# Reciprocal rows spread by transfers, and a rounded query copied by a transfer

## The chip, the cores and the metric

The kernel runs on one core of a Trainium2 chip. The metric is the device time of one execution in microseconds (us), lower is better; the median of several runs is given, and one further execution is profiled.

## The reference, cut to what matters

Three blocks follow each other: decayed causal attention, a mixing block with a two-dimensional Fourier transform and a feed-forward layer, and a second mixing block. The change touches the attention alone, where each row is divided by the sum of its exponentials:

```python
B, H, S, D = 4, 8, 576, 64
scores = scale * np.matmul(q, k.transpose(0, 1, 3, 2))
decay = cum[:, :, :, None] - cum[:, :, None, :]
scores = np.where(causal, -1000000000.0, scores + decay)
scores = scores - np.max(scores, axis=-1, keepdims=True)
attn = np.exp(scores)
attn = attn / (np.sum(attn, axis=-1, keepdims=True) + 1e-09)
out = np.matmul(attn, v)
```

All of it is in 32-bit floats. The 32 pairs of batch and head are the "heads" below; two neighbours make a "pair" (16 pairs).

## The kernel before

**Stages.** `phase1` does the attention and the Fourier transforms of the four batches, `phase2` the feed-forward layer in groups of weights, `phase3` the last block. Where accuracy needs it, a value is split into a rounded high part and a low rest, and the products of the parts are added up in PSUM.

**One head of phase 1.** `load_head` brings raw (128 x 2 x 576: key and query, each twice, on partitions 0 to 63 and 64 to 127) by SP. `prep_units` makes what the score product needs: ACT casts raw into hi; ACT casts the query half of raw into q2 (L251; the tile is called q in the rows), 64 x 576; POOL subtracts twice, for the low part of the query (into hi, L253) and of the key (into kl, L255). Partitions 64 and 65 of q2 and kl carry the decay. `score_units` then does, for each of five blocks of query rows, two matmuls into a bank of PSUM (hi with hi, then q2 with kl), a masked minimum on DVE and an exponential on ACT, which also gives the row sums zs. `turn_units` transposes the exponentials on PE (P to PT), and `av_units` multiplies them by v for both heads of a pair, into one PSUM tile T (pt in the rows) whose partitions 0 to 63 belong to the first head and 64 to 127 to the second; rows of T are features, columns are the 576 queries.

**The division.** With the last block of a pair's second head, ACT adds 1e-9 to the sums, DVE takes the reciprocal rz (128 x 2 x 5), and POOL spreads it to a tile wide, 128 x 5 x 128 (each value 64 times). After the product with v, `spread` turns wide by five transposes on PE, into two banks of PSUM, and ACT copies these in two pieces (448 and 128 columns) to R, 128 x 576, of which there is one buffer. `evac_pair` multiplies T by R on DVE, into X for an even pair and Y for an odd one. After an odd pair one-row transfers (x<-Y, Y<-Y, Y<-x) put the middle features in place; sums and differences of X and Y go to `fft_units` after every fourth pair.

**Order.** `phase1` records the calls up to the turn of the last head and then issues them in an order written out as a string (`ORDERS`), which pins the order of the instructions on each engine, transfers among them. All recorded instructions show as L71 in the trace. What follows is ordered by the framework: the turn of the last head, the spreads of the last two pairs (L326, L327), the last Fourier transform and the first weight loads of phase 2 (L587). Every engine works its own queue in order. SP gives out nearly all transfers of this stage, and a transfer that waits for its input holds those behind it.

Of the kernel before, what the change touches and what calls it, by code (L numbers as in the profile page):

```python
# [8 lines left out]
F32 = mybir.dt.float32  # L9
# [4 lines left out]
ALU = mybir.AluOpType  # L14
# [3 lines left out]
B, H, S, D = 4, 8, 576, 64  # L18
# [4 lines left out]
HT = S // 2 + 1  # L23
# [3 lines left out]
TOP = (0, 66, 192, 320, 448)  # L27
END = (66, 192, 320, 448, 576)
# [25 lines left out]
G = 4  # L54


def f(ap):
    return ap.bitcast(F32)
# [29 lines left out]
class Net:  # L88
# [150 lines left out]
    def prep_units(self, n, pair, raw, hd):  # L239
        nc = self.nc  # L240
        g = n % 2
        kl, q2 = pair["kl"], self.q2[g]
        hi = self.w2.tile([128, 2, S], F32R, tag="hi", name="hi")
        hd["hi"] = hi
        if n == 0:
            nc.scalar.copy(hi[:, 1], raw[:, 1])
            nc.scalar.copy(hi[:, 0], raw[:, 0])
        else:
            nc.scalar.copy(hi, raw)
        yield  # L250
        nc.scalar.copy(q2[0:64], raw[0:64, 1])  # L251
        lows = nc.vector if n == 0 else nc.gpsimd
        lows.tensor_tensor(hi[64:128, 1], raw[64:128, 1], f(hi[64:128, 1]), ALU.subtract)  # L253
        yield
        lows.tensor_tensor(kl[0:64, g], raw[0:64, 0], f(hi[0:64, 0]), ALU.subtract)  # L255
        yield

    def score_units(self, hd, g):
        nc = self.nc
        hi, kl, q2 = hd["hi"], hd["pair"]["kl"], self.q2[g]  # L260
        P = self.P[hd["g"] % 2]
        mn = self.w3.tile([128, 8], F32, tag="mn", name="mn", bufs=2)
        pr = hd["g"] // 2
        zs, rz = self.zs[pr % 2], self.rz[pr % 2]
        hd["P"] = P
        for i in (4, 3, 2, 1, 0):
            end, m0 = END[i], 448 - TOP[i]
            q = slice(TOP[i], TOP[i] + 128)
            ps = self.bank_a()
            pd = self.bank_a() if i == 4 else None  # L270
            parts = [(ps, 0, 448), (pd, 448, end)] if i == 4 else [(ps, 0, end)]
            with self.tc.high_priority(20):
                for t, a, b in parts:
                    nc.tensor.matmul(t[:, 0 : b - a], hi[:, 1, q], hi[:, 0, a:b], start=True, stop=False)
                    nc.tensor.matmul(t[:, 0 : b - a], q2[:, q], kl[:, g, a:b], start=False, stop=True)
                p = P[:, POFF[i] : POFF[i] + end]
                lowest, least = mn[:, i : i + 1], 3.0e38
                for t, a, b in parts:
                    if b < end:
                        to = mn[:, 5:6]  # L280
                    else:
                        to = lowest
                    nc.vector.tensor_tensor_reduce(  # L283
                        out=p[:, a:b], in0=t[:, 0 : b - a], in1=self.mask[:, m0 + a : m0 + b],
                        scale=-0.125, scalar=least, op0=ALU.add, op1=ALU.min, accum_out=to,
                    )
                    least = to
                nc.scalar.activation(p, p, AF.Exp, bias=lowest, scale=-1.0, accum_out=zs[:, g, i : i + 1])
            if i == 0 and g:
                nc.scalar.activation(rz, zs, AF.Copy, bias=1e-9)  # L290
                nc.vector.reciprocal(rz, rz)
                wide = self.w3.tile([128, 5, 128], F32, tag="wide", name="wide", bufs=1)
                each = rz.rearrange("p g i -> p i g").unsqueeze(3).to_broadcast([128, 5, 2, 64])
                nc.gpsimd.tensor_scalar(
                    wide.rearrange("p i (g c) -> p i g c", g=2), each, 1.0, 1.0, ALU.mult, ALU.mult
                )
                hd["pair"]["rz"] = wide
            yield

    def turn_units(self, hd):  # L300
# [18 lines left out]
    def spread(self, p, T, wide):  # L319
        nc = self.nc  # L320
        R = self.c1.tile([128, S], F32, tag="R", name="R", bufs=1)
        for ps, some in ((self.bank_b(), range(4)), (self.bank_a(), (4,))):
            c0 = TOP[some[0]]
            for i in some:
                n = END[i] - TOP[i]
                nc.tensor.transpose(ps[:, TOP[i] - c0 : END[i] - c0], wide[0:n, i], self.ident[0:n, 0:n])  # L326
            nc.scalar.copy(R[:, c0 : END[some[-1]]], ps[:, 0 : END[some[-1]] - c0])  # L327
        return R

    def av_units(self, m, hds, T, wide, done):  # L330
# [733 lines left out]
    def phase3(self):  # L1064
# [58 lines left out]
DIGITS = "#$%&()*+,-./0123456789:;<=>?@ABCDEFGHIJKLMNOPQRSTUVWXYZ[]^_`abcdefghijklmnopqrstuvwxyz|"  # L1123
ORDERS = (
    (
        "&~$6~+X~,e~,e~,e~,e#*35=2)297*+1%)~$$).&|+%/.#$+##///#)-%+(*#)#**#$3<-=[#-811$.T5%;0..252~*p~*p.3361"
        "5#;;4#;*:8,#1>6#*&w;w*()P&***&&l+00G#&.,d+..//,AE=#CJJ?$-@-;-C$,,,,4,,,,,,$+J0##%#$00#%%@2>i#i#%f0%9"
        "#$77:0]/&4//::2/$.?68=#CC/;00-@@>+-0<0./3?#?W,#(,#tu*&&**o.33()H4h#./13#.I&?GN$M@A0C00$F////7//://$."
        "..M#%#$&#G%2$1#%%5%>2=#A&&&9$81(6%00>B#=2//B:A#G,F?/-/=C+@A#,,-FG111)1++#>8#&;&*,,,*+#1+4516#$JCC/4A"
        "4%3@3333%22226222X#)9)$33++O71$5%66&()))6#A6$?D)#((%3(33&(1533$:>:20@$7>-DD./;0,:@@3=..D<D.$//X$)#-5"  # L1130
        "#9(&7)+++)I50#024#$&II$BC,0=$////>/8/<//$.....P$#$##$$$=0#/11%A%%#2D&<<$%%2&#11&F0422=$<1#,A9@-F9E@/"
        "=+.B,A?--G>#F,11]#;@+#&A=--//&.(M+,N&#2:::(18888%>#66H%55555+@5#b))77^,$7#**2*827%)7#6))%=)$G*&:)C,)"
        "F)&8>#=)<77C&B9$55H>+FMM46D26+II$F4::D$7.1),/41,5-4>D?4`BB43@$???$*=-$;pp,oo:n#.l3)620G1e*2.2/1$^)G&"
        "*EX,S((9P+9++#&)#(((&&.&%%%/%%%d#%8%%_%66$5(##%HT,Y0,,22O]$+$$$##+++#*,,$+P#*1**())#5&4#?%2(((<M()%("
        "((C&B&)))&(/-~(Y.^&-GG-&,,FF+-&,,,//*.#-%*++#N*&))C&B)(((&.^*--$,%%**S&)3)00t%(.*R**(lB%&*?(EE&***$S"
        ")8DD99$88(:6>>997@(Q((3(($&&0&&/-&&&&(&7#6FE66?6>%,,3,-?%7=*>%*-**7+++)*A)@BBU)*#)K)))(**P**H())#(#&"
        "%,%&+&&:(9*8**&)#(%$%%J%$$G%x*%%$>s&=&$((9((LHH$MM6NN66&P55b55$>K444@66?6864JJ4IZZI5444Q5PD;;4:9?499"
        "Q9EK4:I8N7M8NN877C7$<J;;C;;J6I;HH;:::GAwwA~%5<?3$~%1>$$~%.0$$9$2$O$$M$$$$+$u#B$(@)F*E>+$D***(9c98AAG"
        "G)77:K_::~$RJ8))$(83((((00((/1W-(((((=)#;&:#9D9FC%..6..%.;.E.%?/>-,CCEE/;,...2<0#=0A-@@D@/$.6111.N%M"
        "74%3.56,52QUCTDc#b/Q1L$__0u+Z%>&)<)D*B)))5)=&((((G%&&&&&&&k:%$0%%%%%%()//#$&&+&$%(#+H+$**D*%)$(($)Z)"  # L1140
        ")$#&7$7%%*$))$(F)(G(&**@$%%*&))%((I%&&3&@%?(((<(@%?-&#X+***DD$)~(8)0+3+++$++(*I+H($FF&&&&E&.&?&&&&;~"
        "$(&(*$T)z%(P((&&&&.&(((&M&?)>E&D****9EE$O999)8;7$>>997@(Q((3((((1$&&/-&&&&(&7#6E66?B6>%,,3,-?%7=*%*-"
        "**78<<+)**))BBK6++)**#)=BGB(A***,,(++)*##(%+&1&&,%+K,*I&#*$%F(($&&A%%$s$$$9%nAA%$$$4>MM4NN6$5eP55886"
        "7773H645444:K_K;4II554V64PPD4:9488>9948DJ:LI8N7M8NN777C7=<<D<3;EJ6I;HH;:::GAA<?3$``~$^>$$0$$38$$O$N$"
        "$$$,$$y#B$(@)*++K<+$*CCi(==8HHLL);;A~$+OcAA~$&N<)~$#)$(73((((/55((6/X(((((A(#?N?#>G>F*%33:3+3E>1C+D5"
        "1110CC110090II22;2#X11/222_W0VVV*RR<$]Q]$l.k-NX|hz~$1-~$0t#JvT#p~$5HR~$3o5G`++#h)C99dIVIIn%xHHHH#GGG"
        "GUGGG/$$-~$W$$$$$$---$,#+N+$###&#/~$8P&%%%#$$~$0$&G#~$C%%%C%+%#$$&&#%#$$$#q%~$.#$$%%#########~$)&&#%"
        "%%$$$$$))$((($&&&&$(I((I(((DD(($A&+++=++++++C&6AH&GM$L**$1))&)))&()&&&&&&,---#,/&.*66-#$$*(+&&#4%3+/"
        "/&%#--+E(+C)/*..E)D),HH;-#,,+++&*2***4**7***7/#5))%((-/)#(($%#$#%%%%##"
    ),  # L1150
)

# [118 lines left out]
```

## Time and profile before

| what | us |
|---|---|
| median of 3 runs | 929.73 |
| lowest and highest | 927.27 to 930.9 |
| the profiled execution's own time | 927.5 |
| its span in the trace | 925.7 |
| attention stage in the written order (L71), ends at about | 231 |
| last Fourier transform, until about | 274 |

The rows below come from the profiled execution. PE is TensorE's matmuls, PEld its weight loads, DVE VectorE, ACT ScalarE, POOL GpSimd, SP SyncE; SPq is the queue from which SP gives out transfers. A row of instructions reads: line, engine, operation, tile written <- tiles read, sizes. Times in brackets are idle time of the engine just before, with what ended it.

### The profile page before, as it was taken

The numbers are of one execution on the slowest core, as the hardware profiler recorded it, in microseconds if no ns is written. First come the engines' busy times: TensorE is split into PE (matmuls) and PEld (weight loads), VectorE is DVE, ScalarE is ACT, GpSimd is POOL, SyncE is SP. The second block draws the span as 40 slices with busy tenths as digits, with TensorE's granted clock in tenths as the row PEclk, the third lists the DMA queues.
The fourth block names the chain that finished last, engine by engine and source line by source line (L and its number), as shares of the span: only waits on it lengthen the run. The fifth ranks groups of instructions, "written<-read, shape, count | busy, mean of one in ns | idle before, by whom it ended". The sixth has DMA issues, their size and how long they took to land.

```text
span 925.7 us, 15855 instructions
## 1 busy us (share of the span) xinstructions
PE 888.4 (96%) x5960; PEld 839.1 (91%) x5960; DVE 604.6 (65%) x1495; ACT 417.7 (45%) x1014; POOL 329.5 (36%) x369
## 2 busy tenths in 40 slices
PE   4999999999698999999999999999999999999998
PEld 3777888878597999999999999999999999999998
DVE  9776787857989635456653665446787747657563
ACT  6898897885535223223221322223335435334331
POOL 6677887987203443000000000000036526435330
PEclk9999999999799999999999999999999999999999
DMA  5743333330323100022232222313300010010001
GB/s 168 217 140 108 121 129 107 110 104 15 110 84 113 47 1 1 4 79 66 80 109 74 91 91 90 142 62 132 100 27 2 1 39 14 14 40 1 26 28 52
DMA packets 23725, 68.04 MB, mean 74 GB/s; under 512 B 2906, under 2 KB 6362, under 8 KB 23648
## 3 DMA queue, kind: packets, MB, share of 16 engines
q1 hardware_dynamic: 20608, 62.88, 20.7%
q0 software_dynamic: 2320, 2.97, 1.2%
q10 hardware_dynamic: 720, 1.18, 0.4%
q8 instruction: 47, 0.77, 0.3%
q14 instruction: 30, 0.25, 0.1%
HBM read 57.91 MB, written 9.07 MB: 72 GB/s over the span
## 4 chain that ended last, share of the span: by engine, by line
PE 58%; DVE 9%; ACT 2%; issue 1%; DMA 0%; POOL 0%; ACTq 0%; DVEq 0%; SPq 0%
PE pa L788 19%; PE pb L802 11%; PE po L802 8%; PE pa L1020 5%; PE pb L1009 5%; PE pa L973 4%; PE po L1009 3%; DVE kra L980 1%; DVE kra L983 1%; DVE kra L982 1%; DVE kra L981 1%; DVE kra L997 1%; DVE kra L979 1%; DVE u L810 1%; PE pa L969 1%
## 5 line engine op out<-in xcount | busy, mean ns | idle before, releaser
L788 PE MATMUL pa<-un,wf 128*128 128x384 f32 x1152 | 220.3, 340 | 7.3 <-ACT un L776 4.4
L788 PEld LDWEIGHTS pa<-un,wf 128*128 128x128 f32 x1152 | 203.7, 191 | 10.4 <-ACT un L776 5.3
L794 DVE SCALAR_TENSOR_TENSOR h<-pa,h 128x384 fp32r<-128x384 f32 x96 | 52.3, 555 | 140.4 <-ACT h L793 140.4
L802 PE MATMUL pb<-h,wf 128*128 128x384 f32 x660 | 133.8, 336 | 0.3 <-DVE u L810 0.3
L802 PEld LDWEIGHTS pb<-h,wf 128*128 128x128 f32 x660 | 116.1, 188 | 1.2 <-DVE u L810 1.0
L793 ACT ACTIVATE h<-pa 128x384 fp32r<-128x384 f32 x96 | 45.7, 489 | 134.2 <-PE pa L788 131.4
L802 PE MATMUL po<-h,wf 128*128 128x384 f32 x492 | 105.4, 339 | 0.4
L965 POOL COPY xd<-u 128x64 f32<-128x64 f32 x32 | 7.3, 266 | 263.7 <-DVE u L810 253.7
L1009 PE MATMUL pb<-wtk,z 128*128 128x288 f32 x513 | 98.3, 295 | 1.6 <-ACT z L998 1.6
L71 ACT ACTIVATE P<-P,mn 128x576 f32<-128x576 f32 (+4 forms) x155 | 86.4, 559 | 16.3 <-DVE mn L71 16.2
L802 PEld LDWEIGHTS po<-h,wf 128*128 128x128 f32 x492 | 86.2, 188 | 3.6 <-ACT h L793 1.5
L999 POOL TENSOR_TENSOR z<-kra,z 128x256 fp32r<-128x256 f32 x72 | 53.2, 753 | 93.8 <-ACT z L998 93.7
L71 PE MATMUL pb<-ident,P 128*128 128x128 f32 (+2 forms) x465 | 81.8, 285 | 4.5 <-DVE PT L71 2.3
L1009 PEld LDWEIGHTS pb<-wtk,z 128*128 128x128 f32 x513 | 79.3, 188 | 2.3 <-ACT z L998 2.3
L71 DVE CUSTOM_DVE_ANT_0 P<-pa,mask 128x448 f32<-128x448 f32 (+3 forms) x155 | 66.3, 454 | 20.3 <-PE pa L71 17.1
L1009 PE MATMUL po<-wtk,z 128*128 128x288 f32 x351 | 75.1, 295 | 0.8 <-ACT z L998 0.8
L71 PE MATMUL pa<-hi 128*128 128x448 f32 (+1 forms) x186 | 65.4, 367 | 1.0 <-DVE mn L283 0.5
L71 PEld LDWEIGHTS pb<-ident,P 128*128 128x128 f32 (+2 forms) x465 | 56.0, 145 | 11.1 <-DVE PT L71 3.9
L973 PE MATMUL pa<-wf,xs 128*128 128x256 f32 x456 | 64.1, 289 | 0.0
L71 DVE COPY PT<-pb 128x448 f32<-128x448 f32 (+1 forms) x93 | 52.9, 594 | 11.7 <-PE pb L71 10.5
L1009 PEld LDWEIGHTS po<-wtk,z 128*128 128x128 f32 x351 | 57.3, 188 | 1.2 <-ACT z L998 1.2
L973 PEld LDWEIGHTS pa<-wf,xs 128*128 128x128 f32 x456 | 57.1, 190 | 0.0
(281 smaller groups left out, 1667.1 us busy)
## 6 DMA issues: line engine op xcount, KB each, us to landing
raw<-in_qk SPq DMA_DIRECT2D x31, 576.0 KB
raw<-in_wf SPq DMA_DIRECT2D x32, 512.0 KB
raw<-in_wtk SPq DMA_DIRECT2D x18, 288.0 KB
v<-in_vp SPq DMA_DIRECT2D x16, 320.0 KB
out<-ob SPq DMA_DIRECT2D x12, 288.0 KB
dft<-in_dft POOLq DMA_DIRECT2D x8, 346.0 KB, 4.8
raw<-in_wth SPq DMA_DIRECT2D x4, 512.0 KB
st_wth<-raw SPq DMA_DIRECT2D x4, 512.0 KB
```

The source lines that it names most:

```text
L71: getattr(getattr(self.nc, engine), name)(*a, **kw)
L788: nc.tensor.matmul(ps[:, 0:CH], t[:, l, 128 * d : 128 * d + 128], un[r][:, d], start=n == 0, stop=n == 11)
L793: nc.scalar.activation(h[:, 0], ps[:, 0:CH], AF.Relu)
L794: nc.vector.scalar_tensor_tensor(h[:, 1], ps[:, 0:CH], 0.0, f(h[:, 0]), ALU.max, ALU.subtract)
L802: nc.tensor.matmul(outs[d], t[:, l, 128 * d : 128 * d + 128], h[:, r], start=k % G == 0 and n == 0, stop=k % G == G - 1 and n == 2,)
L810: nc.vector.tensor_tensor(u[:, d], outs[d], u[:, d], ALU.add)
L969: nc.tensor.transpose(xt[:, 128 * k : 128 * k + 128], src, self.ident)
L973: nc.tensor.matmul(th, xs[:, l, d], self.wth[d][:, r, 256 * hf : 256 * hf + 256], start=n == 0, stop=n == 11)
L979: nc.vector.tensor_scalar(kk, th, INV2PI, MAGIC, ALU.mult, ALU.add)
L999: nc.gpsimd.tensor_tensor(z[:, 1], t, f(z[:, 0]), ALU.subtract)
L1009: nc.tensor.matmul(acc[k][th], z[:, l, 128 * k : 128 * k + 128], self.wtk[kt][:, r, 288 * th : 288 * th + 288], start=first and i == 0 and ...
L1020: self.nc.tensor.matmul(ps[:, 0:288], self.wch[d][:, l, 128 * eo : 128 * eo + 128], us[d][:, r, sl], start=d == 0 and n == 0, stop=d == 3 ...
```

## The change

For every head from the third on, the query half of q2 is no longer cast by ACT but copied by a transfer from hi, on SP. The reciprocals of a pair are transposed once on PE (128 x 10 to 10 x 128), copied by ACT out of PSUM and stored to DRAM by SP as two rows of 640, one per head; POOL's tile wide goes. `spread` is then six transfers on SP from DRAM to R: for each of the two heads, three ranges of columns (66, 126 and 384), each row sent to 64 partitions. The written order is a new string; it covers the new calls.

```diff
-        nc.scalar.copy(q2[0:64], raw[0:64, 1])
+        if n < 2:
+            nc.scalar.copy(q2[0:64], raw[0:64, 1])
+        else:
+            nc.sync.dma_start(f(q2[0:64]), f(hi[0:64, 1]))
...
                 nc.vector.reciprocal(rz, rz)
-                wide = self.w3.tile([128, 5, 128], F32, tag="wide", name="wide", bufs=1)
-                each = rz.rearrange("p g i -> p i g").unsqueeze(3).to_broadcast([128, 5, 2, 64])
-                nc.gpsimd.tensor_scalar(
-                    wide.rearrange("p i (g c) -> p i g c", g=2), each, 1.0, 1.0, ALU.mult, ALU.mult
-                )
-                hd["pair"]["rz"] = wide
+                ps = self.bank_a()
+                nc.tensor.transpose(ps[0:10, 0:128], rz.rearrange("p g i -> p (g i)"), self.ident)
+                turned = self.w3.tile([10, 128], F32, tag="wide", name="rt", bufs=2)
+                nc.scalar.copy(turned, ps[0:10, 0:128])
+                rows = self.fdram.tile([2, 640], F32, tag="rows", name="rows", bufs=2)
+                nc.sync.dma_start(rows.rearrange("g (i q) -> (g i) q", i=5), turned)
+                hd["pair"]["rz"] = rows
...
     def spread(self, p, T, wide):
         nc = self.nc
         R = self.c1.tile([128, S], F32, tag="R", name="R", bufs=1)
-        for ps, some in ((self.bank_b(), range(4)), (self.bank_a(), (4,))):
-            c0 = TOP[some[0]]
-            for i in some:
-                n = END[i] - TOP[i]
-                nc.tensor.transpose(ps[:, TOP[i] - c0 : END[i] - c0], wide[0:n, i], self.ident[0:n, 0:n])
-            nc.scalar.copy(R[:, c0 : END[some[-1]]], ps[:, 0 : END[some[-1]] - c0])
+        for i, n in ((0, 66), (1, 126), (2, 384)):
+            for g in range(2):
+                each = wide[g : g + 1, 128 * i : 128 * i + n].to_broadcast([64, n])
+                nc.sync.dma_start(R[64 * g : 64 * g + 64, TOP[i] : TOP[i] + n], each)
         return R
...
 ORDERS = (
     (
-        "&~$6~+X~,e~,e~,e~,e#*35=2)297*+1%)~$$).&|+%/.#$+##///#)-%+(*#)#**#$3<-=[#-811$.T5%;0..252~*p~*p.3361"
...
+        "&~$8~+_~,l~,l~,l~,l#*35=2)29*+14*%).&+%z/z.#%+#$*&)$//()//%,<-#;E%1#$0:[55#<##U..8.#1611#30-15#40,*#"
...
     ),
 )
```

## Rows read from the trace of the kernel before

**Rows 1.** Busy time, share and instructions of each engine, from the page.

```profile
PE 888.4 (96%) x5960; PEld 839.1 (91%) x5960; DVE 604.6 (65%) x1495; ACT 417.7 (45%) x1014; POOL 329.5 (36%) x369
```

**Rows 2.** Busy time by stretch: span, each engine's busy us (count), clock, DMA.

```profile
31.10:66.30 35.20, 34.29 (x268) 26.71 (x266) 25.05 (x96) 31.69 (x90) 25.43 (x22) 1.00 0.61 183
...
25.00:225.00 200.00, 194.29 (x1521) 162.16 (x1520) 143.68 (x518) 163.32 (x466) 159.90 (x146) 1.00 0.37 118
...
225.00:250.00 25.00, 17.40 (x119) 12.68 (x117) 22.23 (x49) 15.06 (x36) 9.63 (x12) 0.79 0.25 85
...
300.00:925.70 625.70, 619.22 (x4028) 613.23 (x4026) 370.24 (x791) 201.76 (x442) 137.86 (x171) 1.00 0.16 52
```

**Rows 3.** Instruction groups, 25 to 225 us: busy us, mean ns, idle before.

```profile
L71 ACT CAST q<-raw 64x576 fp32r<-64x576 f32 x29 | 19.2, 663 | 0.0
...
L71 ACT COPY R<-pb 128x448 f32<-128x448 f32 x14 | 7.3, 520 | 3.7 <-PE pb L71 3.7
...
L71 ACT COPY R<-pa 128x128 f32<-128x128 f32 x14 | 3.8, 268 | 7.6 <-PE pa L71 5.7 <-DVE Y L71 1.9
...
L71 POOL TENSOR_SCALAR wide<-rz 128x640 f32<-128x640 f32 x15 | 10.9, 726 | 9.4 <-DVE rz L71 6.8 <-DVE mn L71 1.9 <-ACT P L71 0.7
...
L71 PE MATMUL pb<-ident,wide 128*128 128x128 f32 (+2 forms) x56 | 10.0, 266 | 0.2
...
L71 PE MATMUL pa<-ident,wide 128*128 128x128 f32 x14 | 4.2, 303 | 0.0
```

**Rows 4.** Timeline of PE: start, us, instructions merged.

```profile
219.92 1.26 PE L71 MATMUL pb<-ident,P 128*128 128x128 f32 x10 [0.20 <-DVE u L71]
```

**Rows 5.** Waits of PE and of its weight loads, 25 to 225 us: us, times, longest.

```profile
PE pb L71 <- ACT PT L71: 1.3, 2, 0.7
...
PE pb L71 <- ACT P L71: 1.2, 3, 0.8
...
PEld pb L71 <- ACT P L71: 2.1, 4, 1.0
...
PEld pb L71 <- ACT PT L71: 1.1, 2, 0.9
```

**Rows 6.** Timeline of ACT and POOL around one head's cast.

```profile
123.64 1.15 ACT L71 CAST hi<-raw 128x1152 fp32r<-128x1152 f32 x1
...
124.91 1.43 POOL L71 TENSOR_TENSOR hi<-raw,hi 64x576 fp32r<-64x576 f32 x1 [0.21 <-POOL u L71]
...
126.42 1.42 POOL L71 TENSOR_TENSOR kl<-raw,hi 64x576 fp32r<-64x576 f32 x1
```

**Rows 7.** Timeline of SP, which gives out transfers, 123 to 140 us.

```profile
123.87 4.32 SPq L71 DMA_DIRECT2D raw<-in_qk  x2
...
134.06 0.51 SPq L71 DMA_DIRECT2D x<-Y  x1
...
135.75 0.33 SPq L71 DMA_DIRECT2D raw<-in_qk  x1
...
136.24 0.51 SPq L71 DMA_DIRECT2D Y<-Y  x1
...
139.69 0.25 SPq L71 DMA_DIRECT2D Y<-x  x1
```

**Rows 8.** Timeline of the hand-over: SP, DVE and ACT, 228 to 241 us.

```profile
228.99 8.18 SPq L587 DMA_DIRECT2D raw<-in_wf  x3
...
230.49 0.22 DVE L71 RECIPROCAL rz<-rz 128x10 f32<-128x10 f32 x1 [0.24 <-ACT rz L71]
...
232.59 0.67 ACT L601 ACTIVATE a<-raw 128x512 f32<-128x512 f32 x1 [0.99 <-DMA raw<-in_wf]
...
237.29 0.75 DVE L364 TENSOR_TENSOR Y<-pt,R 128x576 f32<-128x576 f32 x1
...
238.07 0.50 SPq L378 DMA_DIRECT2D x<-Y  x1
...
240.48 0.50 SPq L379 DMA_DIRECT2D Y<-Y  x1
```

More of the change, by code (lines that the diff above doesn't have):

```diff
@@ L1125 @@
     (
-        "&~$6~+X~,e~,e~,e~,e#*35=2)297*+1%)~$$).&|+%/.#$+##///#)-%+(*#)#**#$3<-=[#-811$.T5%;0..252~*p~*p.3361"
[L1127 to L1149, printed above, removed]
+        "&~$8~+_~,l~,l~,l~,l#*35=2)29*+14*%).&+%z/z.#%+#$*&)$//()//%,<-#;E%1#$0:[55#<##U..8.#1611#30-15#40,*#"
@@ new lines @@
+        "7,6/,,55#2),91(#7#(%#%%%H4$(~*L~*L--C-))),$+)=*<$)8>>_E$D8(Y$%BBU5575%P6%28L%8$$H0$:$$,0$6$5.$3-$1$="
+        "+$$$,##;#..#--99(,N(N2~$;~$<2+((#.)(22(&2&&44#&&+&#00%%,(&5+&$3*%)H4/$.D(-))j)$++>)*<$)?8>]E$D$X<7%6"
+        "AAR?66&$M63%%I8$$<0$$$,0$66$.$-2>$,$$$$##;#..#>>--(,(2((2)1#&(&446&,&&+#**,*#+(--$..71((()/*.$.&%,,/"
+        "*+AjA.h+---<Db%C=I<H%+::&(DTD8:8)O>)M5)<6&@(3(((/(2(81$&&.?&-&$%%#$$//$.<.)-)4#3+((807)#((3((+66#%(("
+        "(#22&&.()-))$8&0%0G++$*00$/B/$@)-%($8^$%88Y88>%U==85:P7%99L%5%I%14%$$=/$$,$+$*$$$$$$$#28=2+11,,,#+4,"
@@ new lines @@
+        "..#2552+#+6)5))::#-+,,,00//-+#(,--&#4(#3)%*Y,%--0**+A$@-*,,<,$B;;@J$I*9`%&7F[F:77=V=?=6(Q7<(%M&43&I1"
+        "&?&&.&<.$%,%+%%)%%=6&##333.2..9);8/-$#.3,::--+,/0#:-9.#088--03C002*#78+X+2Y2)A+AA/+>$P~$?P==#~$;<<~$"
+        "9);~$7;%:#9~$29~$1999$888&#,,,%+++++#006*55/444*5344#8,#00#&#1111#00&$)%#&&)$33**(%//#<C&%B,:~).??#+"
+        "-<--+,,7,#++*..#-,8)7+#+++++(@@#2.17(#-4--52-CC&0#**#)??<.)<-*++****))0,$++(E(=7=(;;~$&,)+(|*6*S*(P."
+        ".)0-$(+l,(()@g@Ke-(,,a,B)AGG:;;;;>N<)<9;>><+C**7*$)643((((/(.(-(=,((((1#00>0=+/+66.++:39,&++#4**-%@("
@@ new lines @@
+        "*>*%#((;;9M)%))))33)&(#+F++&&&<++&*&)T%(&%%%$))))$$&Bu//C%%$$n<$**j;;$g::%EcE$FJ6I]7==7?<76CCA:6G&5$"
+        "7JDI4HH:6645%E5%@$$$=$/$-$F,$+C$4*$$$$$)#(0((>11(#,55#%,%#$$44;y.)w~%7)(22~%3(/(~%0*6.)$~%+333$&b4%%"
+        "FFt/++q+//,%-k-?<C%<AHH%;+_:&H(GY9:8)$(7;Q(3=%E&&1&&.&22=&0&$%.%%%%*>#$($33#22-1-#,<,7),5$*-*:#9+/++"
+        "0#/-.0.#1+33)44//,/504.+#2370(H5555SS~$765+%3B3#~$/2)1~$,11~$*%0$~$&//~$$////($#000%//4///177/$/###&"
+        "*55#4BB4AA#&?&$%#..($&&,,#)%0<0)$.?$?//-.$-#,,+M1+-/~(n0#/F*,#0,//#.--+,,,#(5,#++)*&/=/#;%AA%#KK+7++"
@@ new lines @@
+        "*//8/*.@*/$-)NOl+)**,*)*3*$=)A(@[C@(~$(((~$%(<(($Q*8*u*O*&L/).(G(j,(+g(()-c-G--A(@FF)$FF99<Y99H;;(<E"
+        ":I<H)G8FSOFNC8B$@A7(F((4$&218&&&.&9&$%%%%%*#66)/$((($6/5$%((1(()9%8))(()<3&;(&&&%%9%%%%*#..~$.$%,&&M"
+        "&&G(~$#F&(Fx&&&&t$%%*p$)))l8$$$B>%=477KK$66JJ38_8N8~%Y67L>36?<6;=6444Y4D6C4BSB5=4<<I4<G49<:;;H4@FH99"
+        "4$B$$1931$$H$/-7$$$$$$jj~$i$$3~$f3#$3~$b3((@((7-~$-6.)(~$)33(*(~$#,K,,-G(BB()q*,,=,l,*DDhFM)LP$O=8<?"
+        "T<<AACA]*D*)K))77)$(0((.V3(2S((+((/(;#-99-83&62==522#D+821<<1000>>+1151+00BB6U211.0U#T/:RR.M.LLmM8kJ"
@@ L1150 @@
+        "M#TJSSScuu~$,~$,Io$nHall~$0#~$/lvvv*^jt~$eO$~$$MM~$`#L~$^Lbk~$ZLLLh~$V$K~$T#JJJlJJjJ%#~$P#f#######%%"
+        "~$U,#<++$####%%%#$$&&#6%#$$$#%%%#$$$$##%~$0%%#$$$#%%#$u$$$~$*$$##n))#(((&&&&&#*%)#((##%%%V%#$&&&&&??"
+        "&&#><<%%*9***6***;*#)8#7/=#<))#((=%<())%(()****&*(55.<4;)%993Q,%O&&.&%&%/1**-**.@.+--B%A#FFJ:I?,,$+;"
+        "+>#&#((((#6&7&#5#$$2#######+$$&$#%%###"
     ),
```

## Prediction

> **What bounds the kernel now.** I read the page's engine totals first [rows 1], then the busy time by stretch [rows 2], because a share over the whole span mixes three stages. Two rows settle where to look [rows 2]. From 300 us to the end PE's matmul time is 619.2 of 625.7 us and its weight loads 613.2: that part is a stream of large matmuls, and the change touches nothing in it. What it can move lies ahead of 300 us: the attention stage, which runs up to about 231 us in the written order (L71 in the rows), and the hand-over that follows it, where PE is busy 17.4 of 25 us and the granted clock is 0.79 on the mean, against 1.00 (its level of 2.4 GHz) in the stage before.
>
> In the stretch 25 to 225 us PE looks full (194.3 of 200 us), ahead of ACT (163.3), POOL (159.9) and DVE (143.7) [rows 2]. That reading needs a correction. A transpose is listed with 266 ns for the spread's own [rows 3], yet ten transposes in a row took 1.26 us [rows 4]: the first shows its full length of about 0.28 us and each further one adds (1.26 - 0.28) / 9 = 0.109 us. So busy time on PE overstates what a removed matmul gives back by 2.4 times, and PE has gaps inside its "busy" time. In the part of the stage that has no Fourier work yet (31.1 to 66.3 us) ACT is busy 31.7 of 35.2 us, 90%, and PE's weight loads 26.7 [rows 2]. My reading: PE and ACT share the bound here, each waiting for the other now and then; the waits of PE that ended on ACT's tiles P and PT add up to 1.3 + 1.2 + 2.1 + 1.1 = 5.7 us in 200 us [rows 5].
>
> **The change part by part.**
>
> *ACT.* It loses the cast into q, 29 x 663 ns = 19.2 us in the stretch, and the two copies into R of each pair, 7.3 + 3.8 = 11.1 us [rows 3]. It gains one copy of a 10 x 128 tile out of PSUM per pair. No row has that shape; the nearest is the 128 x 128 copy into R at 268 ns, and I take it whole: 15 x 0.27 = 4.1 us. Net: 19.2 + 11.1 - 4.1 = 26.2 us less in 200. On top of that ACT stood idle 3.7 + 7.6 = 11.3 us ahead of the R copies, since they waited at the head of its queue [rows 3]; the new copy waits for one transpose instead, so part of this goes too.
>
> *PE.* 56 + 14 = 70 transposes of the wide tile go, 15 transposes of the reciprocals come: 55 fewer. At 0.109 us each that is 6.0 us; by listed durations it would be 55 x 0.27 = 14.9 us, which I reject for the reason above.
>
> *POOL.* 15 x 726 ns = 10.9 us less [rows 3], and the 9.4 us that it sat idle ahead of them goes in part. POOL is not the bound (159.9 of 200), so I count nothing.
>
> *The query copy.* The transfer starts when the cast into hi has ended and must land before the score matmuls of that head. Those matmuls also need the low parts that POOL makes after the same cast: cast over at 123.64 + 1.15 = 124.79, kl over at 126.42 + 1.42 = 127.84, so 3.05 us later [rows 6]. Small transfers on the same queue give the price: Y<-Y was issued 2.2 us after x<-Y, on which it waits (134.06 to 136.24) [rows 7]; in the hand-over the same step took 2.41 us (238.07 to 240.48) [rows 8]. So an undisturbed copy (2.2 to 2.4 us, somewhat more for its 64 x 2304 bytes) hides behind POOL, and I cost it at nothing. It loses that cover if it stands behind a load: Y<-Y issued right after a raw load (135.75, 136.24) released the next step only at 139.69, 3.45 us later [rows 7]. Then 3.45 - 3.05 = 0.4 us per head shows, 29 x 0.4 = 11.6 us at worst. The lower end is zero, because the same matmuls wait for kl in any case.
> The Trainium skill, page "DMA: Bandwidth & Descriptors", section "Queues, rings and completion order", speaks against this part: transfers given out by one engine share that engine's rings, and each DMA engine takes the entries of a ring in order, so a short copy stays behind a long load. The 3.45 against 2.41 us agrees with it. By that rule alone, with every copy behind a load, the sum below would be 11.6 us worse.
>
> *The rows and the spread.* Per pair one store of 10 x 128 and six reads of 64 partitions, all on SP, which is free but works in order. An issue costs 0.33 us on SP (the raw load at 135.75 [rows 7]), so with two query copies nine new issues take 3.0 us of a pair's 12 or so. The reciprocals are ready an iteration or two before the spread needs them, and R is free as soon as the product of the pair before is done, so the two latencies (2.4 us store, 1.65 us of issue and 2.4 us of landing) have about one pair's time to hide in. I cost them at nothing in the middle of the stage. Behind a waiting transfer in SP's queue stand the raw loads of the next heads: the load issued at 123.87 [rows 7] would land, with the 3.6 us that the first weight load took (228.99 to 232.59 [rows 8]), at 127.5, and its cast began at 129.61, so it has 2.1 us to spare. The transfers add 29 x 147 KB + 14 x 295 KB = 8.4 MB to the stretch, 42 GB/s on top of 118; the DMA engines' share would go from 0.37 to about 0.37 x 160 / 118 = 0.50, no bound.
>
> *The written order.* The string can't be turned into times by reading it. I bound it from both sides: it could give nothing, or it could give all that ACT is relieved of, 26.2 us. I take PE's 6.0 us in full, since PE runs nearest to full, and half of the 5.7 us that PE waits for ACT, 2.9 us. That makes 8.9 us, nearer to PE's end because PE's rows are nearer to the limit (194.3 against 163.3).
>
> *The hand-over.* The last reciprocal starts at 230.49, the last product Y at 237.29 [rows 8]. After: 230.49 + 0.20 (reciprocal) + 0.30 (transpose) + 0.27 (copy) = 231.26; store 2.4, to 233.7; five issues of 0.33 ahead of the last, 1.65, and 2.4 to land: 237.7. That is 0.4 us late. What follows Y is a chain of one-row transfers and the last Fourier work, so a delay counts in full. If SP holds these reads behind the third of the weight loads in [rows 8] (its group ends at 237.17), they land at 237.17 + 1.65 + 2.4 = 241.2, 3.9 us late. If the product comes earlier because R's transposes no longer stand in PE's line, a gain of 1 us is the most I see. Bounds -1 to +3.9; I take +1, nearer to the undisturbed sum.
>
> **Sum.** -8.9 + 1.0 = -7.9, say 8 us. The profiled execution took 927.5 us (span 925.7), 2.2 us under the median of 929.73; 927.5 - 8 = 919.5, and on the median 929.7 - 8 = 921.7 us.
>
> **The rivals.**
>
> *A, the forecast:* PE's share and half of its waits for ACT: 921.7 us, 915 to 926 with the bounds of the hand-over and of the ACT part (6.0 to 11.7 us gained).
>
> *B, ACT was the real bound.* For it: 90% busy without Fourier work, and 11.3 us idle ahead of R inside its own queue. Against it: PE has about 97% by listed time, and the new order can't press PE below its own work. Half-way between 8.9 and 26.2 is 17.6, less 1 for the hand-over: 929.7 - 16.6 = 913 us.
>
> *C, the gain goes nowhere.* The stage's pace is then set by chains that the change leaves alone, such as the score product on DVE, its exponential and POOL's low parts. For it: POOL is busy 160 of 200 us, and ACT also has idle time. Against it: PE loses real work. Gain 0 to 4, hand-over +1: 926 to 931, middle 928.5.
>
> *D, SP's queue takes it back and more.* Place: a transfer of rows or R waits at the head of SP's queue for its input, and the raw load behind it comes late. Price: 3.0 us of issues and 1.0 us of ring delay (3.45 - 2.41), less 2.1 us to spare, is 1.9 us for a pair; at half of the 15 pairs 14 us. With A's gain and the hand-over: 929.7 - 8.9 + 14 + 1 = 936 us. It decides from the point at which a load is held up by more than 2.1 us in most pairs. For it: there are two raw buffers, so a load can be given out only when POOL is done with the head before, and it has nothing in hand. Against it: an order made with queued transfers in view can put the loads ahead.
>
> **How the numbers follow.** A 0.48, B 0.14, C 0.20, D 0.18. A difference of 0.5%, 4.6 us (about what a measurement of this kernel can tell from none), puts the line at 925.1 and 934.4. Faster: B and nearly all of A, 0.60. Within: C and the rest of A and a little of D, 0.23. Slower: most of D, 0.17. The range that leaves out no more than 2 in 10 runs from the far part of B to the middle of D: 910 to 936. A's own range is 915 to 926.
>
> **What would show it.** In 25 us stretches of the attention stage: ACT's busy share lower by about a tenth, PE's weight loads denser, and the last product Y some 8 us earlier than the 237.29 of before. The query cast and both R copies gone from ACT; score matmuls still released by POOL's kl and not by the query transfer (against D). Raw loads followed by their casts without ACT idling for a transfer; if ACT or PE shows waits on a transfer into q or raw, D holds. In the hand-over Y should come about 7 to 8 us after the last reciprocal; 11 us would be the late end of its bound. The prediction is wrong if the attention stage doesn't get shorter although ACT is relieved (C), or if it gets shorter by over 15 us (B).

## The result

The changed kernel took 938.74 us (median of 7 runs, 933.17 to 940.55) against 927.69 us for the kernel before, measured beside it; the ratio is 1.0106 with a 95% interval of 1.008 to 1.0133. The change made the kernel about 1% slower. The forecast was 921.7 us, with 936 as the upper end of its range: the sign was wrong and the range missed by 2.7 us.

The profiled execution of the changed kernel took 938.9 us, with a span of 937.1 us against 925.7. Its page shows less work on ACT and POOL than [rows 1], and more transfers; their row in the kernel before follows:

```profile
PE 890.0 (95%) x5896; PEld 838.1 (89%) x5896; DVE 607.3 (65%) x1495; ACT 396.4 (42%) x968; POOL 315.3 (34%) x353
...
DMA packets 34126, 77.28 MB, mean 82 GB/s; under 512 B 9179, under 2 KB 14843, under 8 KB 34049
```

```profile
DMA packets 23725, 68.04 MB, mean 74 GB/s; under 512 B 2906, under 2 KB 6362, under 8 KB 23648
```

Three marks split the 11.4 us. The last reciprocal rz starts at 237.71 us instead of 230.49 [rows 8]: 7.2 us lost in the attention stage. The last product Y follows 13.5 us later instead of 6.8: another 6.7 us in the hand-over. From Y to the end it is 685.9 us instead of 688.4, so 2.5 us come back. The busy time by stretch (span, then busy us of PE, PEld, DVE, ACT and POOL, granted clock, DMA share, GB/s), after the change:

```profile
25.00:50.00 25.00, 19.59 (x116) 16.57 (x117) 13.32 (x49) 15.10 (x50) 12.71 (x13) 0.87 0.74 197
25.00:225.00 200.00, 184.57 (x1408) 151.76 (x1409) 138.25 (x491) 138.37 (x410) 139.94 (x123) 0.97 0.55 161
225.00:250.00 25.00, 20.36 (x159) 15.62 (x158) 22.10 (x61) 14.09 (x35) 15.79 (x19) 0.97 0.28 92
250.00:275.00 25.00, 20.88 (x100) 18.28 (x101) 22.18 (x43) 12.66 (x26) 2.28 (x2) 0.69 0.28 102
```

Against [rows 2], ACT is 25 us less busy in 25 to 225 us, as forecast. PE got through 1408 matmuls against 1521; 55 of the difference are the transposes taken out, the other 58 are work that came later. In these 200 us no engine is busier; all of them wait more. Some of it shows at the start of the stage. The timeline of SP, POOL, DVE and PE there (start, us, instruction, idle time before it):

```profile
32.97 4.81 SPq L71 DMA_DIRECT2D R<-rows  x6
...
36.26 1.45 POOL L71 DMA_DIRECT2D dft<-in_dft  x2 [0.84 <-ACT dft L71]
...
43.07 0.76 DVE L71 TENSOR_TENSOR X<-pt,R 128x576 f32<-128x576 f32 x1 [6.28 <-DMA R<-rows]
...
44.43 0.38 PE L71 MATMUL pa<-ident,rz 128*10 128x128 f32 x1 [5.11 <-DVE mn L71]
```

The six spreading transfers of the first pair take SP 4.8 us, and while they move, POOL gives out the Fourier tables dft. DVE, and behind it PE, stand still for over 5 us. The waits of the whole stage (25 to 235 us: total us, times, longest):

```profile
POOL hi L71 <- ACT hi L71: 41.7, 14, 6.4
...
DVE X L71 <- DMA R<-rows: 6.3, 1, 6.3
ACT hi L71 <- DMA raw<-in_qk: 5.4, 5, 1.6
DVE Y L71 <- DMA R<-rows: 3.9, 1, 3.9
...
PE pa L71 <- DMA q<-hi: 1.6, 3, 1.0
```

POOL, which waited 8.4 us for ACT's cast in the same stretch before, waits 41.7. But it waits 35.1 us in the kernel below that leaves the spreads out, where the stage is 15 us shorter, so this wait doesn't measure the loss. The four rows that name R, raw or q add up to 17 us (with all the smaller ones for transfers, 27), but some are long and most pairs have none: the list names a few places and doesn't explain the pace. SP's own timeline between them shows more:

```profile
59.14 0.30 SPq L71 DMA_DIRECT2D rows<-rt  x1
59.53 0.36 SPq L71 DMA_DIRECT2D raw<-in_qk  x1
60.23 0.58 SPq L71 DMA_DIRECT2D Y<-Y  x1
60.93 1.79 SPq L71 DMA_DIRECT2D R<-rows  x3
63.24 0.50 SPq L71 DMA_DIRECT2D q<-hi  x1
63.81 1.85 SPq L71 DMA_DIRECT2D R<-rows  x3
65.76 0.38 SPq L71 DMA_DIRECT2D kl<-scr  x1
66.24 0.36 SPq L71 DMA_DIRECT2D raw<-in_qk  x1
```

One spread costs SP 0.6 us (median of 84: 594 ns), a query copy 0.5, a raw load 0.35 (0.33 in the kernel before). From the rows' store to the next raw load SP issues for 7 us with short gaps only. POOL's kl, the last to read the raw buffer, ended at 64.89; the next load went out at 66.24. It is so in much of the stage. With each of the 27 raw loads from 25 to 235 us set against the end of the kl that frees its buffer, the median load goes out 0.03 us after it in the kernel before, and 5 go out more than 1 us after it; in the changed kernel the median is 1.36 us, and there are 15 such loads. SP's own waits in this stretch, in the changed kernel and then in the kernel before:

```profile
SPq L71 <- ACT rt L71: 29.7, 14, 6.0
...
SPq L71 <- POOL kl L71: 7.5, 4, 2.9
```

```profile
SPq L71 <- POOL kl L71: 25.8, 15, 3.5
```

All waits of SP add up to 96 us, against 186 before. So SP isn't giving out transfers all the time: for 30 us the store of the rows stands at the head of its queue and waits for ACT's copy rt, with the loads behind it. That wait alone isn't the loss, for it is 25 us in the kernel without spreads too.

In the hand-over (SP, DVE):

```profile
237.71 0.21 DVE L71 RECIPROCAL rz<-rz 128x10 f32<-128x10 f32 x1
...
239.26 0.30 SPq L71 DMA_DIRECT2D rows<-rt  x1
241.82 4.03 SPq L329 DMA_DIRECT2D R<-rows  x5
245.96 0.53 SPq L589 DMA_DIRECT2D raw<-in_wf  x1
246.53 0.45 SPq L329 DMA_DIRECT2D R<-rows  x1
...
251.18 0.76 DVE L366 TENSOR_TENSOR Y<-pt,R 128x576 f32<-128x576 f32 x1 [1.33 <-DMA R<-rows]
```

Five spreads take 4.0 us to give out (one of them 1.6 us), a weight load of 512 KB goes out before the sixth, and the sixth lands behind it.

### The profile page after: what moved, and what is told of

Same layout as the page of the kernel before. It is cut to its first block, busy times and chain, and to the rows that moved or that the text cites. A ratio compares the mean times of both kernels' runs of the same rounds, so it can differ in the third digit from the quotient of the medians.

```text
span 937.1 us, 15941 instructions
## 1 busy us (share of the span) xinstructions
PE 890.0 (95%) x5896; PEld 838.1 (89%) x5896; DVE 607.3 (65%) x1495; ACT 396.4 (42%) x968; POOL 315.3 (34%) x353
## 4 chain that ended last, share of the span: by engine, by line
PE 63%; DVE 8%; DMA 3%; ACT 2%; issue 2%; POOL 1%; SPq 1%; ACTq 0%; DVEq 0%; POOLq 0%
PE pa L790 19%; PE pb L804 12%; PE po L804 9%; PE pb L1011 6%; PE pa L1022 5%; PE pa L975 4%; PE po L1011 4%; DMA raw<-in_wf 2%; PE pb L71 1%; DVE kra L982 1%; DVE a L610 1%; PE pa L971 1%; DVE a L608 1%; DVE kra L985 1%; DVE kra L984 1%
## 5 line engine op out<-in xcount | busy, mean ns | idle before, releaser
L804 PE MATMUL po<-h,wf 128*128 128x384 f32 x492 | 107.3, 344 | 3.4 <-DVE h L796 2.1
L71 POOL TENSOR_TENSOR hi<-raw,hi 64x576 fp32r<-64x576 f32 x30 | 42.5, 1417 | 47.1 <-ACT hi L71 42.8
```

What stands on the lines that cost most here:

```text
L71: getattr(getattr(self.nc, engine), name)(*a, **kw)
L804: nc.tensor.matmul(outs[d], t[:, l, 128 * d : 128 * d + 128], h[:, r], start=k % G == 0 and n == 0, stop=k % G == G - 1 and n == 2,)
```

## The experiments

Where a kernel keeps the changed order, calls that are left out or replaced keep their places in it. "rz" and "Y" are the starts of the last reciprocal and the last product (before 230.49 and 237.29, after 237.71 and 251.18). The kernel before took 927.3 to 929.7 us beside them. Differences in us are between medians; by the ratios some are up to 2.3 us smaller.

The theories. At first three: **L**, the spreading transfers land late at a few places (the first pair, pair 5, the hand-over); **Q**, the new issues on SP's queue hold up the raw loads behind them; **O**, the new written order is slower by itself. After the first four kernels: **S**, the loss is made at the start, where transfers land behind the Fourier tables and the clock then falls; **I**, Q put as a price for each issue on SP, in every pair; and **R**, the late landing of the spreads themselves, whoever issues them.

**The query copy alone**, in the kernel before, with its own order:

```diff
-        nc.scalar.copy(q2[0:64], raw[0:64, 1])
+        if n < 2: nc.scalar.copy(q2[0:64], raw[0:64, 1])
+        else: nc.sync.dma_start(f(q2[0:64]), f(hi[0:64, 1]))
```

> The kernel before with the query copy alone: for heads 2 to 31 the cast into q on ACT becomes a transfer on SP at the same place of the order of before; spread and order stay as before. Three theories for the slow result. L: the spread's transfers land late, at the first pair (DVE waited 6.3 us for R), at pair 5 (3.9 us) and in the hand-over (13.5 us from the last reciprocal to the last product, against 6.8). Q: SP's queue, with query copies and spread issues in it, holds up the raw loads of the next heads. O: the new written order is by itself slower. L expects this kernel at 922 to 927 us, since ACT is relieved of 19 us and nothing is spread by transfers. Q expects 930 or more. O expects 927 or less.

936.58 us, 1.0097 [1.0073, 1.012]; rz 236.81, Y 243.98. The part that I had costed at nothing loses nearly as much alone as the whole change. Raw loads go out as promptly as before (median 0.03 us), so Q has the number and not the place. The timeline at the start and the stretches there (columns as above), then the same stretches of the kernel before:

```profile
36.56 1.50 POOL L71 DMA_DIRECT2D dft<-in_dft  x2 [1.30 <-ACT dft L71]
36.74 0.34 SPq L71 DMA_DIRECT2D raw<-in_qk  x1
38.09 0.47 SPq L71 DMA_DIRECT2D q<-hi  x1
44.85 0.82 PE L71 MATMUL pa<-kl,q 66*128 66x448 f32 x2 [2.83 <-DMA q<-hi]
...
40.00:45.00 5.00, 1.83 (x13) 1.38 (x12) 2.64 (x9) 2.51 (x8) 4.30 (x5) 0.86 1.14 315
45.00:50.00 5.00, 5.00 (x21) 3.49 (x22) 2.31 (x10) 2.40 (x9) 1.68 (x2) 0.50 0.67 184
```

```profile
40.00:45.00 5.00, 4.50 (x34) 3.60 (x34) 4.96 (x22) 4.83 (x15) 4.44 (x6) 1.00 1.08 333
45.00:50.00 5.00, 4.92 (x48) 3.56 (x44) 2.00 (x10) 3.80 (x12) 2.12 (x2) 1.00 0.74 216
```

A copy issued at 38.09, behind a raw load on SP's queue and beside tables of 346 KB each on POOL's, released PE at 44.85, 6.8 us later. PE waited 2.83 us for it; during this wait the granted clock fell, and from 45 to 50 us it was 0.50 (1.2 GHz): 21 matmuls in 5 us where there had been 48, though not all the same ones.

**The copy only from head 8 on**, when the tables are loaded (`if n < 8` in the same edit):

> The kernel before, with the query copied by a transfer only from head 8 on; heads 2 to 7, which are prepared while the Fourier tables are loaded, keep ACT's copy. Theory S (the loss of the query transfers is made once, at 42 to 50 us, where the transfer lands 2.8 us late behind the 256 KB tables and TensorE then works at a granted clock of 0.50): the 9 us of the kernel with all query transfers are gone, 926 to 930 us, last reciprocal at 229.5 to 231.5 us, granted clock 1.00 in 45 to 50 us. Rival I (every issue of about 0.5 us on SP and every late landing costs): two thirds to nine tenths of the loss stay, 933 to 936 us.

932.34 us, 1.0051 [1.0038, 1.0063]; rz 230.97, Y 237.81. In the stage 5.8 of the 6.3 us are gone, and the clock in 25 to 50 us is 1.00: the copies of six heads made that loss, the other 24 heads 0.5 us. The total fell short of that (about 3 us stay behind Y), and why was not settled.

**The work that the change takes from the engines simply left out**: the query's rounding from head 2 on, POOL's spread, the transposes and the copies into R (R is a constant), in the order of before.

> The kernel before with the work simply left out that the change moves to transfers: no cast into q from head 2 on, no wide tile on POOL, no transposes and copies into R (the product takes a constant tile); order of before. It shows what relieving ACT, PE and POOL is worth if nothing took its place. My sum said 8.9 us in the stage, so 918 to 920 us or less with the hand-over's own relief. If the stage's pace is set by what stays, 925 to 927.

923.52 us, 0.9955 [0.994, 0.9969]; rz 229.96, Y 236.92; between the two expectations. With all this work gone the stage is 0.5 us shorter; in the traces most of the gain falls behind Y (2.5 us), and why is open. What ACT gained it waits for now: its exponentials of this kernel, and of the kernel before (busy us, mean ns, idle before them in 25 to 225 us):

```profile
L79 ACT ACTIVATE P<-P,mn 128x320 f32<-128x320 f32 (+4 forms) x149 | 82.6, 556 | 32.0 <-DVE mn L79 31.8
```

```profile
L71 ACT ACTIVATE P<-P,mn 128x320 f32<-128x320 f32 (+4 forms) x149 | 83.0, 558 | 16.0 <-DVE mn L71 15.9
```

So neither ACT nor those transposes set the pace in the order of before.

**The changed kernel without the 96 spreading transfers** (R is a constant; all else stays, query copies too):

> The changed kernel without the 96 transfers into R; the product takes a constant tile, so the division is left out. The stores of the reciprocals and the query transfers stay. L expects all of the waits on R back, 6.3 + 3.9 in the stage and 6.7 in the hand-over: about 922 us. Q expects part of it, from the 3.6 us of SP issues in a pair: 925 to 932. O expects the stage as long as in the changed kernel (last reciprocal near 237 us) and only the hand-over shorter: 932.

919.37 us, 0.99 [0.9875, 0.9926]; rz 222.60, Y 231.70; below what any of the three theories expected. The new order together with the relief holds a gain of 7.9 us in the stage (the order without the relief was not run); the spreads take that back and as much again, 15 us, and 19.4 in all. Without them raw loads go out as promptly as in the kernel before (median 0.03 us).

**The last two pairs, 14 and 15, spread in the old way** in the changed kernel:

> The changed kernel, but the last two pairs (14 and 15, whose spread stands in the hand-over) go the old way: POOL's wide tile, five transposes, two copies by ACT. L expects the hand-over's 6.7 us back: 938.7 - 6.7 = 932 us, and 6 to 8 us from the last reciprocal to the last product. Q and O, which put the loss in the stage before, expect 937 to 940.

934.7 us, 1.0079 [1.0052, 1.0106]; rz 235.71, Y 244.18. From rz to Y it is 8.5 us instead of 13.5, and 4 us of the total come back (2.5 by the ratios, whose intervals overlap). Without spreads it was 9.1 us, so of the 6.7 us lost there about 4.5 belong to the transfers, and some 2 remain without them.

**The query on ACT again, in the changed kernel** (the first edit undone):

> The changed kernel with the query's rounding back on ACT for every head; the reciprocals still go through DRAM with six transfers and the new order stays. Theory S: the first pair's product still waits over 5 us for its reciprocals and TensorE's clock still falls in 25 to 50 us, so 935 to 941 us. Rival (the query transfers are what costs in the new order too): 928 to 932 us.

936.74 us, 1.0101 [1.0066, 1.0136]; rz 233.50, Y 246.21. The number fits, the place doesn't: PE is busy 24.0 us in 25 to 50, so the first pair is not late here. A wait of 5.2 us for R follows in 50 to 75 us, with a granted clock of 0.86. Nor does theory I explain it: SP is rid of the same 30 issues here as in the kernel below that has them on ACT's queue, and raw loads go out about as late (median 0.70 us and 0.65), yet 2.0 us come back here and 9.0 there. ACT is busy 16 us more in 25 to 225 us than in the changed kernel (154.5 against 138.4); whether its casts cost the other 7 us was not tested.

**The old way at both ends**: ACT's copy for heads 2 to 7, and pairs 0, 14 and 15 spread by POOL, PE and ACT.

> The changed kernel with the old way at the two ends: ACT copies the query of heads 2 to 7, and pairs 0, 14 and 15 spread their reciprocals by POOL, TensorE and ACT; 13 pairs go through DRAM. Theory S (the loss sits at the start and at the hand-over): last reciprocal at 228 to 232 us, the last product 6 to 9 us behind it, 924 to 929 us. Rival I (78 issues of 0.59 us on SP hold up the raw loads in every pair): last reciprocal at 233 us or later, 932 us or more.

929.94 us, 1.0036 [1.0012, 1.0059]; rz 232.53, Y 240.99. The number lies between the two theories: the ends hold 9 of the 11 us (6.5 of 9.8 by the ratios), yet the stage is still 10 us longer than without spreads (222.60). So the 78 transfers in the middle cost something too, unless the old way at the ends costs it in this order, which was not measured. (This kernel and the one with pairs 14 and 15 have one buffer for the turned reciprocals instead of two.)

**Two spreads for a pair instead of six**, each 64 x 640, and the product on DVE in three pieces:

```diff
-        R = self.c1.tile([128, S], ...)
-        for i, n in ((0, 66), (1, 126), (2, 384)):
-            for g in range(2):
-                each = wide[g : g + 1, 128 * i : 128 * i + n].to_broadcast([64, n])
-                nc.sync.dma_start(R[64 * g : 64 * g + 64, TOP[i] : TOP[i] + n], each)
+        R = self.c1.tile([128, 640], ...)
+        for g in range(2):
+            nc.sync.dma_start(R[64 * g : 64 * g + 64], wide[g : g + 1].to_broadcast([64, 640]))
```

> The changed kernel with two transfers of 64x640 for a pair instead of six of 64x66, 64x126 and 64x384, and the product in three pieces on DVE. SP issues four fewer a pair, 4 x 0.59 = 2.4 us, 38 us in all. Rival I: raw loads go out sooner in every pair, 928 to 933 us. Theory S: the first pair's transfers still land late behind the tables and the last pair's behind the 512 KB load, 934 to 938 us.

929.1 us, 1.0015 [0.9997, 1.0033]; rz 227.48, Y 236.69. As theory I has it, 64 issues fewer give back 9.6 us, and raw loads go out 0.18 us late instead of 1.36 (medians), though the bytes are a little more and PE still waits once, 3.9 us, for a query at the start.

**The same with four dead spreads behind the two**, of 64 x 66 into a tile that nobody reads:

```diff
+        pad = self.c1.tile([64, 4, 66], F32, tag="pad", name="pad", bufs=1)
+        for i in range(4):
+            nc.sync.dma_start(pad[:, i], wide[0:1, 0:66].to_broadcast([64, 66]))
```

> The kernel with two spreading transfers of 64x640 for a pair, and behind them four more of 64x66 into a tile that nobody reads: SP issues six a pair again, as in the changed kernel, but no result waits for four of them. Theory I (the time that SP's queue spends on issues holds up the raw loads and the query copies behind): the gain of the two transfers is gone, 935 to 940 us. Rival R (what cost was the product's wait for the last of six late transfers): it stays, 928 to 932 us.

945.09 us, 1.0171 [1.014, 1.0203]; rz 243.72, Y 252.79. No result waits for these four, and they cost 16 us, 1 us a pair: against R, and more than I had it. (The kernel is also 6 us slower than the changed one, which has as many issues; that is not explained.) SP's timeline at one pair, and two waits of the stage (25 to 235 us) that were 3.2 and 3.9 us without the dead spreads:

```profile
98.11 0.48 SPq L79 DMA_DIRECT2D q<-hi  x1
98.70 1.18 SPq L79 DMA_DIRECT2D R<-rows  x2
99.93 2.50 SPq L79 DMA_DIRECT2D pad<-rows  x4
```

```profile
ACT hi L79 <- DMA raw<-in_qk: 10.4, 5, 3.8
PE pa L79 <- DMA q<-hi: 8.8, 5, 3.6
```

The dead issues hold SP for 2.5 us, and what comes later on SP's queue, the raw loads and query copies, is what PE and ACT wait for. The median raw load goes out 1.51 us late, against 0.18 without them. The load of the DMA engines hardly differs: their share in 25 to 225 us is 0.58 against 0.56.

**The 30 query copies issued on ACT's queue** in the changed kernel, right behind ACT's cast; the six spreads stay on SP:

```diff
-            nc.sync.dma_start(f(q2[0:64]), f(hi[0:64, 1]))
+            nc.scalar.dma_start(f(q2[0:64]), f(hi[0:64, 1]))
```

> The changed kernel with the 30 query copies issued on ACT's queue, right behind ACT's own cast that they read; SP issues 30 x 0.5 = 15 us less and never waits for the cast. Theory I: at the rate of the step from six to two spreads (9.6 us of time for 38 us of issues) 3 to 5 us, and more where SP had waited for the cast with a raw load behind: 930 to 936 us. Rival (the query's transfers cost by their late landing, whoever issues them): 937 to 941 us.

929.73 us, 1.0012 [0.9991, 1.0033]; rz 230.15, Y 243.08. The same bytes moved, in as many transfers, and 9.0 us came back from moving 15 us of issues to another queue, more than the 3 to 5 us expected at the least. SP's and ACT's queue at one pair:

```profile
57.10 0.36 SPq L71 DMA_DIRECT2D raw<-in_qk  x1
...
58.22 3.94 SPq L71 DMA_DIRECT2D R<-rows  x6
...
59.50 0.47 ACTq L71 DMA_DIRECT2D q<-hi  x1
```

The query copy goes out at 59.50 while SP is still giving out spreads. The Trainium skill, page "DMA: Bandwidth & Descriptors", section "Issuing engines are not separate DMA queues", says that issuing from several engines saves only the sequencer's issue time, usually small beside the transfer. That a second queue saves time agrees: one issue takes 0.47 us here, and moving 30 of them gave 9 us in all. That it is the issue time alone which gave them, no run shows.

**The six spreads issued on POOL's queue** (`nc.gpsimd.dma_start` in `spread`):

> The changed kernel with its six transfers issued on POOL's queue instead of SP's. SP's queue is rid of 96 issues, and of the waits in front of them. Theory I: raw loads go out as soon as their buffer is free, last reciprocal at 227 to 231 us, 927 to 932 us, if POOL's own work (six issues of some 0.7 us a pair) stays hidden. Rival R: the transfers land as late as before, 936 to 942 us.

961.33 us, 1.0359 [1.033, 1.0388]; rz 265.91, Y 280.57. Both theories missed. POOL's group of spreads and waits for POOL, 25 to 235 us:

```profile
L71 POOL DMA_DIRECT2D R<-rows x79 | 41.5, 529 | 13.5 <-DMA rows<-rt 11.6 <-DVE Y L71 1.7
```

```profile
PEld pa L71 <- POOL kl L71: 9.2, 8, 2.1
PE pa L71 <- POOL kl L71: 7.0, 6, 1.8
```

POOL spends 41.5 us giving them out and stands 11.6 us in front of them until the rows have landed, with the low parts kl, on which PE's scores wait, behind. In these two runs a second queue helped where the transfer's input is made on the same engine just before (ACT's cast), and not where it waits for another transfer; what POOL's 41.5 us of issues cost by themselves was not told apart.

**One spread of 128 x 640 for a pair**, alone and with ACT's copy for heads 2 to 7:

```diff
+        nc.sync.dma_start(R, wide.unsqueeze(1).to_broadcast([2, 64, 640]))
```

> One transfer of 128x640 for a pair instead of six, product in three pieces. Theory I: against the two transfers another issue of 0.56 us fewer in each of 16 pairs, 9 us of SP's queue, of which a fifth to a third shows as in the step from six to two (9.6 us of time for 38 us of issues): 926 to 928 us, 0 to 3 below two transfers. Rival R: no change against two, 929 us.

> One transfer of 128x640 for a pair, and the query's rounding of heads 2 to 7 on ACT, by transfer from head 8 on. If the loss at the start (a query that lands late behind the tables, then a halved clock; 4 to 5 us) and the loss on SP's queue add up: 921 to 925 us, below the kernel before. If ACT's six casts cost at the start what the transfers cost: 926 to 929 us.

998.36 us, 1.0753 [1.0722, 1.0784], and 994.78 us, 1.0708 [1.0675, 1.0742]; both theories missed by 70 us. A stretch in which such a transfer moves (columns as above), and waits of the first of the two, 25 to 235 us:

```profile
72.00:73.00 1.00, 1.00 (x12) 0.50 (x10) 0.86 (x2) 1.00 (x6) 1.00 (x2) 1.00 0.13 49
```

```profile
PE pa L79 <- DMA q<-hi: 15.3, 3, 6.2
DVE Y L79 <- DMA R<-rows: 14.3, 2, 7.3
```

The DMA share is 0.13, two of 16 engines; in the kernel with two spreads it was 0.95 from 59 to 61 us, with spreads, a raw load and a query copy given out shortly before. The transfer becomes slow, and the query copies and loads behind it as well. This agrees with the Trainium skill, same page, section "Rules for kernel authors", that an outermost dimension below 16 confines a transfer to that many engines; here the outermost dimension of the source is 2.

**Two spreads joined with the other remedies**: ACT's copy for heads 2 to 7, query copies on ACT's queue, or both.

> Two spreading transfers of 64x640 for a pair, and ACT's copy of the query for heads 2 to 7. The 3.9 us wait of TensorE for a query at the start goes, and the clock stays at 1.00 in 25 to 50 us: 923 to 927 us. If the start's loss is made good later anyway: 928 to 930 us.

> Two spreading transfers of 64x640 for a pair, and all 30 query copies issued on ACT's queue. Theory I: 924 to 928 us. Rival (late landing, whoever issues): 928 to 931 us, with the wait of 3.9 us for a query at the start as before.

> As the one before, with ACT's own copy of the query for heads 2 to 7. If the causes add up: 920 to 924 us, below the kernel before by over 0.5%. If not: 925 to 929 us.

927.26 us, 0.999 [0.9973, 1.0006]; 929.94 us, 1.0018 [0.9996, 1.004]; 927.78 us, 0.9987 [0.9971, 1.0002]. The two reliefs of SP's queue don't add up: either gives 9 us, both give no more, and the 924 to 928 us that theory I expected of them is missed. With two spreads there is little left to relieve: in all three kernels the median raw load goes out 0.03 us late. With ACT's copy at the start the stage is well ahead of the kernel before (rz 223.74 and 225.70, Y 232.97 and 234.88), but the whole is not faster. For the first of these, the stretch from 295 to 305 us, and the same of the kernel before:

```profile
295.00:305.00 10.00, 9.04 (x37) 8.71 (x38) 6.82 (x11) 1.83 (x5) 4.73 (x4) 0.66 0.35 105
```

```profile
295.00:305.00 10.00, 10.00 (x60) 9.50 (x59) 8.52 (x15) 3.84 (x8) 6.60 (x5) 1.00 0.35 106
```

In the opening of phase 2, PE has idle gaps in both kernels, and here one more stretch follows with the clock at 0.66: 37 matmuls against 60. Of the 4.3 us by which Y was early, 1.2 are left in the span. That is seen in one trace each; that the clock is what eats every such gain was not tested. No complete kernel was measurably faster than the one before.

## Why the prediction was wrong

**ACT's relief, right in size.** 26.2 us less in 200 were forecast, 24.9 were measured (163.3 to 138.4); the copy out of PSUM took 244 ns, not 268.

**The stage, -8.9 us, wrong reason and wrong sign.** I took it from removed transposes and from PE's waits for ACT, for any order. The relief alone gave 0.5 us in the stage in the order of before, where the work waits for DVE's minimum: rival C's mechanism. The new order without spreads is 7.9 us ahead, so a gain of about that size was there to have, but it takes the new order and an SP queue without the spreads; that the sum had this size is luck.

**"I cost them at nothing in the middle of the stage": the step that failed.** I priced every new issue at 0.33 us, the row of a raw load [rows 7]. A spread to 64 partitions took 0.59 and a query copy 0.50, so nine issues cost 0.30 + 2 x 0.50 + 6 x 0.59 = 4.8 us for a pair instead of 3.0. And I asked whether the transfers' own latency had time to hide, not what SP's time costs those behind: raw loads went out 1.36 us late on the median instead of 0.03. The spreads cost 15 us in the stage; four dead ones, 2.5 us of SP's time a pair, cost 1 us a pair; taking 15 us of issues off SP gave 9 where they went to ACT's queue, but 2 where ACT cast instead. The DMA engines' load was right (a share of 0.55 against 0.50, 161 GB/s against 160), and no bound. Which of the transfers behind hurts most is open: the listed waits for transfers explain part of the loss, the rest is spread over ACT and POOL waiting for each other. That raw loads go out late is shown; whether they and the query copies also move more slowly, for their place in SP's rings, is not, since moving a transfer to another queue changes both.

**The query copy at nothing, wrong at the start.** The cover of 3.05 us by POOL's low part holds in the middle in the order of before: 24 heads cost 0.5 us. With the spreads on the same queue it isn't shown to hold, for there the copies' move to ACT's queue gave 9.0 us. The worst case that I set, 0.4 us for a head behind a load, was read in the middle, where no tables move. Beside the tables a copy took 6.8 us, and the idle time cost PE its clock: 5.8 us from six heads.

**The hand-over, +1 us (at most +3.9), measured +6.7.** From rz to the store 1.55 us against 0.77; from the store to the first spread 2.56 against 2.4, right; five issues 4.03 against 1.65; the sixth given out behind a weight load, and landing 4.65 us after its issue (246.53 to 251.18) against 2.4. About 2 us were not from the transfers. I had seen the weight loads ahead of the spreads as the late case; they came between them.

**The rivals.** D was right in sign and, at 936 us, close in size; its place, SP's queue with raw loads late behind the spreads, is where the runs point. The size was partly luck. Its price rested on the issue cost of 0.33, and on late raw loads alone; only 5 waits of ACT, 5.4 us, name a raw load. With the 4.8 us of issues that were measured, the same working gives 28 us instead of 14, and 950 us in all. A was right in what it saw (a gain near 8 us in the stage) and blind to what the same queue would charge for it. A's range of 915 to 926 comes out of the profiled 927.5 us; from the median that its 921.7 goes by, the same bounds give 917 to 928, which the result misses as well.

## What to carry to other kernels

An in-order queue that looks free in the profile can have a price for each issue: take it from a row with the same shape of transfer, add it up for the transfers that somebody waits for behind it, and count small transfers first, since joining six into two gave 9.6 us and moving 30 to the queue of the engine that makes their input gave 9.0 (both together no more). Where a short copy takes the place of an engine's work, look at every stretch for what else is moving, above all at the start where tables are loaded; a wait of 2.83 us there cost nearly as much again in clock (an estimate: half of the next 5 us, at 0.50). And leave the work out first: the kernel without it showed 4 us to gain where the sum had 8.

## What the runs showed of the hardware that I had not expected

- The issue cost on SP follows the shape: 0.30 us for a store of 10 rows, 0.35 for a load of 128 partitions, 0.50 for an SBUF copy of 64 partitions, 0.59 for a row sent to 64 partitions (medians in the changed kernel). With the dead spreads a row of 66 columns took 0.60 and one of 640 columns 0.58.
- A transfer whose source has an outermost dimension of 2 ran at a DMA share of 0.13 (72 to 73 us); DVE waited up to 7.3 us for it, and PE up to 6.2 us for a query copy.
- After PE had waited 2.83 us its granted clock was 0.50 for the next 5 us; by that estimate the wait cost almost twice its length.
- Transfers given out by POOL took 0.53 us of POOL's time each, and one that waits for an earlier transfer held POOL's arithmetic for up to 5.8 us.
